# A state-space scan beside local attention on one core: the chunk scan for several state groups at once, the skip term added on eviction, softmax's maximum and sum by TensorE, and a new order

## The chip, the core and the metric

The kernel runs on one core of a Trainium2 chip. A core has five engines that run side by side, each with its own list of instructions: TensorE (PE in the profile; PEld is its weight load), VectorE (DVE), ScalarE (ACT), GpSimd (POOL) and SyncE (SP). Matmuls write to PSUM, and another engine has to copy ("evict") them from there to SBUF. DMAs are issued by an engine's instruction stream and land some microseconds later. The metric is the device time in microseconds (us), lower is better.

## The reference

Two independent layers on 2048 positions of 448 features; their outputs stand side by side. Layer A is a diagonal state-space recurrence with 448 complex states, layer B is causal, dilated local attention with 16 heads of 28 features, a window of 8 and a dilation of 2.

```python
def _A_ref(x, Lambda_re, Lambda_im, B_re, B_im, C_re, C_im, log_dt, Dskip):
    Lam = Lambda_re + 1j * Lambda_im
    Lam_bar = jnp.exp(jnp.exp(log_dt) * Lam)
    B_bar = ((Lam_bar - 1.0) / Lam)[:, None] * (B_re + 1j * B_im)
    Bu = jnp.einsum("bld,pd->blp", x + 0j, B_bar)
    for t in range(L):
        h = Lam_bar[None, :] * h + Bu[:, t, :]
        hs.append(h)
    return 2.0 * jnp.einsum("blp,dp->bld", hseq, C_re + 1j * C_im).real + x * Dskip[None, None, :]

def _B_ref(x, wqkv, wo):          # H = 16 heads, Dh = 28, W = 8, dilation 2
    q, k, v = ...                  # x @ wqkv by heads
    idx = pos[:, None] - (jnp.arange(W) * dil)[None, :]
    logits = jnp.einsum("bhsd,bhswd->bhsw", q, kg) * Dh ** -0.5   # kg, vg: k, v gathered at idx
    logits = jnp.where(mask, logits, -1e9)
    o = jnp.einsum("bhsw,bhswd->bhsd", softmax(logits), vg)
    return o.reshape(B, S, D) @ wo

out = jnp.concatenate([a, b], axis=-1)     # bf16, [1, 2048, 896]
```

## The kernel before

**How the order comes about.** The program is first described as a list of units, each with an engine (or a choice of ACT or VectorE), a cost, and the units it depends on. A table of numbers, `ORDER`, then gives the order in which the units are written out, and with it each engine's list of instructions; `BANKS` gives the PSUM buffer of each unit that needs one. So what stands ahead of an instruction on its engine is fixed by these tables. PSUM holds two tiles of two banks (ring "W") and four of one bank (ring "s").

**Layer A.** The 2048 positions are 128 chunks of 16. States come in seven groups of 64, real and imaginary parts on 128 partitions. The setup computes powers of the transition (exponential and sine on ACT, small VectorE operations up to L942), a table of turns per chunk (L952 to L967), and the folded input matrices Bcat (L996). The scan then does for each group m in turn:

- input matmuls into `scP` (two banks, positions 0 and 2 of every four) and `scb` (two single banks, 1 and 3), L1063;
- a short tree over the 16 positions of a chunk: ACT copies `eP` (L1076), matmul L1080, copy `e1` (L1084), matmul L1087, copy `eG` (L1091), matmuls L1095 to L1097. The last 128 columns of `scb` are then the sum over each chunk;
- the scan over the 128 chunks on VectorE: each column is turned by the table into a frame where the transition is real (L1103 to L1106, four instructions), scanned (L1107) and turned back into `pbuf` (L1109 to L1112). Nine instructions on 128 columns for each group;
- the carry of each chunk's start into its positions: matmuls L1117, L1123, L1124 and L1163 on PSUM that still holds its own part or is given it again by an ACT copy (L1131, L1149: "seed"), and evictions to `h`.

The output y is seven matmuls of 448 columns for each of the 16 positions (L1244), in pairs of positions in one W tile. An ACT copy puts the skip term, x times Dskip (product on VectorE, L1227), in the tile beforehand (L1256), the matmuls add to it, and ACT or VectorE evicts it.

**Layer B.** x comes by DMA transposes and the projection weights by loads (`load`, `wload`). Half of the weights are copied to the other half of the partitions (`shift`, L240) so that odd features can be multiplied. `proj` (L493) projects K and Q in two halves of 1024 positions, evicted by ACT or VectorE; Q's eviction scales. For a third block of columns two pieces are moved by DMAs on the SP queue (L555, L556). Fourteen products of q and shifted k (L578, 128x4096 on VectorE) go through matmuls that sum over a head's features into logits (L592). Softmax, once for each half: maximum over the window (L611), subtraction (L612), exponential on ACT (L618, ahead of it a table load L617), sum (L623), reciprocal (L624), product (L626), then a small merge (L635) and a transpose (L640). The attention weights are expanded on VectorE (L698, sixteen of 128x2176), multiplied with V on TensorE (`o_ps`, L709 and L714), evicted to oT, multiplied with wo (L734) and written out.

**Queues.** The SP queue issues x of both layers, then the wv weights, the moves of the third block and the outputs. The ACT queue issues the Q and K weights and two of A's three parameters; log_dt goes on SP between B's transposes.

Of the kernel before, what the change touches and what calls it, by code (L numbers as in the profile page):

```python
# [40 lines left out]
NHO = 3  # L41
NF = 3
# [3 lines left out]
ORDER = [  # L46
# [24 lines left out]
]  # L71
BANKS = [
# [154 lines left out]
class Ctx:  # L227
# [41 lines left out]
    def consts2(self):  # L269
# [38 lines left out]
        def masks():  # L308
            G.memset(mrow[:], 0.0)
# [6 lines left out]
        self.u_mask = self.plan.add("POOL", 1.5, masks, [self.boot], 1)  # L316
# [438 lines left out]
class PartA:  # L755
# [83 lines left out]
    def setup(self):  # L839
# [110 lines left out]
        def t1():  # L950
# [6 lines left out]
            for c in (6.28125, 1.9353071795864769e-03):  # L957
                V.scalar_tensor_tensor(a[:], k, -c, a[:], op0=ALU.mult, op1=ALU.add)
# [420 lines left out]
```

## Time and profile before

| | us |
|---|---|
| three runs | 141.83, 141.04, 143.16 |
| median | 141.83 |
| the profiled execution | 141.83 |
| its span | 139.8 |
| its mean granted TensorE clock | 0.988 of full speed |

The span is what the profile covers; 2.03 us of the profiled execution lie outside of it. The profile's stages, VectorE's timeline, the groups and the waits are shown with the prediction.

### The profile page before, as it was taken

To read this page: it belongs to the slowest core of one execution; us is meant where nothing else is said; L and a number is where in the kernel's file an instruction comes from. 1 tells how busy PE (TensorE), PEld (TensorE's weight loads), DVE (VectorE), ACT (ScalarE), POOL (GpSimd) and SP (SyncE) were. 2 spreads that over 40 slices of the span, in tenths; PEclk is the share of its full clock that TensorE was granted. 3 is DMA by queue.
4 is the path that set the end of the run, shared out by engine and by line. 5 is a ranking of instruction groups with operands and counts; after the bars stand their busy time and mean duration, and the time that the engine had idled before them with its cause. 6 is when DMAs were issued, how large, how long until landed. Compare 5 with 4: busy or idle time off the path is not lost.

```text
span 139.8 us, 2787 instructions
## 1 busy us (share of the span) xinstructions
PE 126.5 (91%) x1079; PEld 62.0 (44%) x1079; DVE 108.7 (78%) x176; ACT 105.8 (76%) x162; POOL 8.7 (6%) x46
## 2 busy tenths in 40 slices
PE   6499999999999999989897799799997999979980
PEld 2165753644343343543434355446454545535530
DVE  1348999999998999999999999999979748110360
ACT  0346999999999989679597989799986957545510
POOL 7890000000000000000000000000000000000000
PEclk9959999999999999999999999999999999999999
DMA  4999991796453458703600000300179272203345
GB/s 91 260 244 171 223 114 38 172 209 83 93 111 66 96 148 130 119 0 85 150 0 0 0 5 0 99 0 5 10 220 266 71 225 90 86 0 99 99 158 171
DMA packets 36484, 14.69 MB, mean 105 GB/s; under 512 B 26615, under 2 KB 36471, under 8 KB 36471
## 3 DMA queue, kind: packets, MB, share of 16 engines
q1 hardware_dynamic: 35549, 13.71, 45.3%
q10 hardware_dynamic: 922, 0.81, 2.3%
q8 instruction: 8, 0.13, 0.4%
q14 instruction: 5, 0.04, 0.1%
HBM read 5.57 MB, written 3.67 MB: 66 GB/s over the span
## 4 chain that ended last, share of the span: by engine, by line
PE 56%; DVE 19%; ACT 13%; issue 5%; SPq 4%; DMA 0%; DVEq 0%; ACTq 0%
PE y_ps L1244 14%; PE qk_ps L493 12%; PE wo_ps L734 6%; PE scb L1063 4%; PE scP L1063 4%; ACT qk L236 4%; SPq L390 4%; DVE prods L698 4%; DVE turned L1105 3%; DVE turned L1111 3%; ACT qk L238 3%; PE v_ps L664 3%; ACT V L236 2%; DVE turned L1107 2%; PE logits L592 2%
## 5 line engine op out<-in xcount | busy, mean ns | idle before, releaser
L578 DVE TENSOR_TENSOR prods<-qk 128x4096 bf16<-128x4096 bf16 x14 | 31.5, 2286 | 1.0 <-ACT qk L238 0.7
L493 PE MATMUL qk_ps<-rb 128*128 128x256 bf16 (+2 forms) x132 | 24.0, 338 | 2.1 <-DMA prm<-in_A_log_dt_dram 2.0
L698 DVE TENSOR_TENSOR prods<-at,band 128x2176 bf16<-128x2176 bf16 x16 | 19.9, 1285 | 0.0
L493 PEld LDWEIGHTS <-rb 128*128 128x128 bf16 (+1 forms) x132 | 11.5, 102 | 12.1 <-issue 6.9
L734 PE MATMUL wo_ps<-wo_p,oT 128*128 128x448 bf16 x64 | 14.4, 352 | 0.0
L1244 PE MATMUL y_ps<-Ccat,qk 128*128 128x448 bf16 x60 | 13.8, 352 | 0.0
L240 DVE CAST qk<-y_ps 128x896 bf16<-128x896 f32 (+1 forms) x4 | 3.9, 975 | 12.6 <-PE y_ps L1244 7.3
L1063 PE MATMUL scb<-xaT_sb,Bcat 128*128 128x512 bf16 (+1 forms) x56 | 13.6, 381 | 0.0
L1063 PE MATMUL scP<-xaT_sb,Bcat 128*128 128x512 bf16 (+1 forms) x56 | 13.6, 380 | 0.0
L664 PE MATMUL v_ps<-wv,rb 128*128 128x448 bf16 (+1 forms) x64 | 13.2, 353 | 0.2 <-ACT V L236 0.2
L1063 PEld LDWEIGHTS <-Bcat 128*128 128x128 bf16 (+1 forms) x112 | 8.6, 97 | 10.6 <-issue 3.6
L236 ACT CAST qk<-wo_ps 128x448 bf16<-128x448 f32 x12 | 6.5, 548 | 8.8 <-PE wo_ps L734 8.8
L1244 PE MATMUL y_ps<-Ccat,rb 128*128 128x448 bf16 x45 | 11.0, 353 | 0.0
L236 ACT CAST qk<-qk_ps 128x512 bf16<-128x512 f32 (+3 forms) x13 | 8.8, 693 | 1.2 <-PE qk_ps L493 1.2
L238 ACT ACTIVATE qk<-qk_ps 128x1024 bf16<-128x1024 f32 (+3 forms) x10 | 8.4, 857 | 0.6 <-PE qk_ps L493 0.6
L236 ACT CAST oT<-o_ps 128x512 bf16<-128x512 f32 x14 | 7.8, 606 | 1.2 <-PE o_ps L714 1.2
L734 PEld LDWEIGHTS <-oT 128*128 128x128 bf16 x64 | 6.2, 98 | 5.6 <-issue 0.5
L1244 PEld LDWEIGHTS <-qk 128*128 128x128 bf16 x60 | 5.9, 98 | 5.5
L664 PEld LDWEIGHTS <-rb 128*128 128x128 bf16 (+1 forms) x64 | 4.9, 96 | 6.7 <-issue 3.7
L236 ACT CAST V<-v_ps 128x448 bf16<-128x448 f32 x16 | 7.8, 545 | 0.1
L592 PE MATMUL logits<-prods,Zsel 128*32 128x512 bf16 (+1 forms) x112 | 7.5, 382 | 0.0
L1256 ACT CAST y_ps<-xaT_sb 128x896 f32<-128x896 bf16 x8 | 7.3, 914 | 0.2
(163 smaller groups left out, 212.0 us busy)
## 6 DMA issues: line engine op xcount, KB each, us to landing
out_dram<-qk SPq DMA_DIRECT2D x18, 112.0 KB, 2.0
xaT_sb<-in_A_x_dram SPq DMA_DIRECT2D x4, 448.0 KB, 5.7
out_dram<-qk SPq DMA_DIRECT2D x7, 224.0 KB, 2.1
rb<-in_B_wqkv_dram ACTq DMA_DIRECT2D x2, 336.0 KB, 4.0
wv<-in_B_wqkv_dram SPq DMA_DIRECT2D x2, 336.0 KB, 4.3
qk<-qk SPq DMA_DIRECT2D x4, 128.0 KB
bX<-in_A_B_re_dram SPq DMA_DIRECT2D x1, 392.0 KB
bX<-in_A_B_im_dram SPq DMA_DIRECT2D x1, 392.0 KB, 5.8
```

The source lines that it names most:

```text
L236: nc.scalar.copy(out, in_)
L238: nc.scalar.mul(out, in_, scale)
L390: nc.sync.dma_start(self.xB[:, b, j], x[256 * (4 * b + j):256 * (4 * b + j + 1)].rearrange("(n e) d -> n (e d)", e=2), transpose=True)
L493: nc.tensor.matmul(out(e)[:, NCH * j0:NCH * j1], lhsT=w, rhs=self.xB[rows, b, j0:j1, c, :], start=e not in begun, stop=True, skip_group_ch ...
L578: V.tensor_tensor(p, q[:, :, t0:t0 + HB].unsqueeze(1).to_broadcast([NCH, 4, 2, HB]), bass.AP(k.tensor, k.offset, [k.ap[0], [2, 4], [LDK, 2 ...
L592: nc.tensor.matmul(lg[32 * i:32 * i + 32, 4 * xx:4 * xx + 4, :], lhsT=sel[:, H - H * r:3 * H - H * r], rhs=pr[rows, :, g // 4, NCH * (g % ...
L664: nc.tensor.matmul(box[e][:], lhsT=self.xB[rows, b, jj, c, :], rhs=self.wv[rows, c, :], start=e not in begun, stop=True, skip_group_check= ...
L698: V.tensor_tensor(p.rearrange("p (g r v) -> p g r v", g=16, v=W), self.at[b][:, 64 * e + 16 * g:64 * e + 16 * g + 16].unsqueeze(2).to_broa ...
L734: nc.tensor.matmul(ps[:], lhsT=self.oT[:, ub["r"], kt, NCH * m:NCH * m + NCH], rhs=self.wo_p[:, kt, :], start=(kt == 0), stop=(kt == KT - 1))
L1063: mt(ps(i), lhsT=lhsT, rhs=rhs, start=i not in begun, stop=True, **kw)
L1244: nc.tensor.matmul(ps, lhsT=self.pb[:, m, PAD:] if j + jj == T - 1 else self.h[m][:, i, g * NCH:(g + 1) * NCH], rhs=self.Ccat[:, m, :], st ...
L1256: nc.scalar.copy(jb["y"][:, :, 0:D], self.xd[j])
```

## The change

- **The scan in two phases.** Part 1 does the input matmuls and the tree for each group and leaves the own parts in `h` straight away (no separate `eP`, `e1`, `eG`); the chunk sums go to a tile `sums` in fp32 by an ACT copy. `chunks(0, 4)` then turns, scans and turns back four groups at once, `chunks(4, 7)` the other three: turns are four instructions on 512 or 384 columns, the scan stays one instruction for each group. Part 2 does the carry of each group: an ACT copy seeds PSUM from `h` again, or (for three groups' two-bank part) VectorE adds PSUM to `h` (L1155). `h` of the first four groups has a tile of its own; that of the others lies in rb. Ccat moves into rb, oT into qk's region.
- **The skip term** is added by VectorE as it evicts y (L1244), and all of these evictions are VectorE's; the eight ACT copies go.
- **Softmax.** The maximum is kept in bf16 and subtracted by two matmuls with minus the identity; the sum is eight matmuls with the identity into `sm_ps`, which the reciprocal reads.
- **The table of turns** is made with fewer passes, and its sine with another scale.
- **Start.** All A parameters go on the ACT queue, and the Q weights on the SP queue behind four of B's transposes. K's projection of the first half is split by transposed block, the weight copies are three for each kind, and 13 warm-up matmuls stand where there were 10.
- **Order and banks** are new throughout.

```diff
-WARM = 10
-FIN = (("seed", "seed"), ("seed", "seed"), ("seed", "seed"), ("hold", "seed"), ("seed", "seed"), ("seed", "seed"), ("hold", "hold"))
+NB = 4
+WARM = 13
+FIN = (("add", "seed"),) * 3 + (("seed", "seed"),) * 4
...
-        self.more = lambda: nc.scalar.dma_start(self.wqk[:, 0:3, 0:D],
-                                                self.B_wqkv[0:DF, 0:D].rearrange("(k p) c -> p k c", p=NCH))
+        nc.sync.dma_start(self.wqk[:, 0:3, 0:D], self.B_wqkv[0:DF, 0:D].rearrange("(k p) c -> p k c", p=NCH))
...
         def top():
-            V.tensor_tensor(lg[:], lg[:], box["mx"][:].unsqueeze(1).to_broadcast([NCH, W, NCH]), op=ALU.subtract)
+            box["mx"] = pool.tile([NCH, NCH], bf16, name="mx", tag="mx")
+            V.tensor_reduce(box["mx"][:], self.lg[b][:].rearrange("p w q -> p q w"), axis=AX.X, op=ALU.max)
+
+        def sub():
+            for k in range(2):
+                nc.tensor.matmul(self.lg[b][:, 4 * k:4 * k + 4, :], lhsT=cx.minus[:],
+                                 rhs=box["mx"][:].unsqueeze(1).to_broadcast([NCH, 4, NCH]), start=False, stop=True,
...
+        def add():
+            box["sm"] = self.psum.tile([NCH, NCH], f32, name="sm_ps", slot=s_sm)
+            for w in range(W):
+                nc.tensor.matmul(box["sm"][:], lhsT=cx.ident[:], rhs=box["e"][:, :, w], start=(w == 0), stop=(w == W - 1))
+
         def norm():
-            V.tensor_reduce(sm[:], box["e"][:], axis=AX.X, op=ALU.add)
-            V.reciprocal(sm[:], sm[:])
+            V.reciprocal(sm[:], box["sm"][:])
...
-            V.tensor_scalar(k, a[:], 1.0 / TWO_PI, MAGIC, op0=ALU.mult, op1=ALU.add)
-            V.tensor_scalar(k, k, MAGIC, None, op0=ALU.subtract)
-            for c in (6.28125, 1.9353071795864769e-03):
-                V.scalar_tensor_tensor(a[:], k, -c, a[:], op0=ALU.mult, op1=ALU.add)
+            V.tensor_scalar(k, a[:], MAGIC, MAGIC, op0=ALU.add, op1=ALU.subtract)
+            V.tensor_tensor(a[:], a[:], k, op=ALU.subtract)
...
+        def chunks(m0, m1):
+            k = m1 - m0
+            x, u, w = xs[:, m0:m1], sc[:, 0, 0:k], sc[:, 1, 0:k]
+            tc, ts = (self.tab[:, i, m0:m1] for i in range(2))
+
+            def turn(out, op):
                 V.tensor_tensor(u, x, tc, op=ALU.mult)
+                for a, b in ((lo, hi), (hi, lo)):
                     V.tensor_tensor(w[a], x[b], ts[b], op=ALU.mult)
+                V.tensor_tensor(out, u, w, op=op)
+
+            def fore():
+                turn(u, ALU.add)
+                for i in range(k):
+                    V.tensor_tensor_scan(x[:, i], self.o["ex"][:, m0 + i, NLP:NPW].to_broadcast([NCH, NCH]), u[:, i], 0.0,
+                                         op0=ALU.mult, op1=ALU.add)
...
+                    if mode == "add":
+                        V.tensor_tensor(dst, src(box[name]), dst, op=ALU.add)
...
+        for m0, m1 in ((0, NB), (NB, NM)):
+            for m in range(m0, m1):
+                part1(m)
+            chunks(m0, m1)
+        for m in range(NM):
+            part2(m)
...
-                cx.copy(eng, o, jb["y"][:, j0:j1, 0:D])
-
-            def seed(j=j, jb=jb):
-                jb["y"] = self.psum.tile([NCH, 2, 512], f32, name="y_ps", slot=jb["s"])
-                nc.scalar.copy(jb["y"][:, :, 0:D], self.xd[j])
+                nc.vector.tensor_tensor(o, jb["y"][:, j0:j1, 0:D], self.xd[j][:, j0:j1], op=ALU.add)
...
-            en = lambda n: (("ACT", "DVE"), (act(n) + 0.13 * (n > 512), vec(n)))
+            en = lambda n: ("DVE", vec(n))
```

The order shows what moved. VectorE ahead of the first products (`prods<-qk`), before; `sh` to `spair`, `pw` and `Gd` are A's setup:

```order
L958 SCALAR_TENSOR_TENSOR ang_232<-tab,ang_232 128x896 x2
L924 TENSOR_TENSOR sh<-sh 128x84
L925 TENSOR_SCALAR sh<-sh 128x84
L927 TENSOR_TENSOR la<-sh,pex 128x14
L929 TENSOR_SCALAR la<-la,turn 128x7 x2
L931 TENSOR_TENSOR ab<-la,ll 128x28
L934 TENSOR_TENSOR gs<-ab 128x2x7x2
L937 TENSOR_TENSOR spair<-pex,sh 128x42x2 x2
L1012 TENSOR_TENSOR pw<-Dm,spair 128x640
L942 TENSOR_TENSOR Gd<-Dm,gs 128x896
L578 TENSOR_TENSOR prods<-qk 128x4096
```

The same place now, where lines have new numbers:

```order
L931 TENSOR_TENSOR Dm<-ident 128x64
L583 TENSOR_TENSOR prods<-qk 128x4096 x2
L937 TENSOR_TENSOR sh<-sh 128x84
L938 TENSOR_SCALAR sh<-sh 128x84
L940 TENSOR_TENSOR la<-sh,pex 128x14
L942 TENSOR_SCALAR la<-la,turn 128x7 x2
L944 TENSOR_TENSOR ab<-la,ll 128x28
L947 TENSOR_TENSOR gs<-ab 128x2x7x2
L950 TENSOR_TENSOR spair<-pex,sh 128x42x2 x2
L1024 TENSOR_TENSOR pw<-Dm,spair 128x640
L955 TENSOR_TENSOR Gd<-Dm,gs 128x896
```

Two products stand ahead of that part of the setup, and the passes of the table of turns stand further back. VectorE around a chunk scan, before, where `turned` is the scratch tile:

```order
L578 TENSOR_TENSOR prods<-qk 128x4096
L1103 TENSOR_TENSOR turned<-scb_764,tab 128x128
L1105 TENSOR_TENSOR turned<-scb_764,tab 64x128 x2
L1106 TENSOR_TENSOR turned<-turned 128x128
L1107 SCALAR_TENSOR_TENSOR turned<-pex,turned 128x128
L1109 TENSOR_TENSOR turned<-turned,tab 128x128
L1111 TENSOR_TENSOR turned<-turned,tab 64x128 x2
L1112 TENSOR_TENSOR pbuf<-turned 128x128
L1012 TENSOR_TENSOR pw<-Dm,spair 128x640
```

And now, with the scratch in qk's region, up to the second softmax (`mx` its maximum, `sm` its reciprocal):

```order
L583 TENSOR_TENSOR prods<-qk 128x4096 x2
L1113 TENSOR_TENSOR qk<-sums,tab 128x512
L1115 TENSOR_TENSOR qk<-sums,tab 64x512 x2
L1116 TENSOR_TENSOR qk<-qk 128x512
L1121 SCALAR_TENSOR_TENSOR sums<-pex,qk 128x128 x4
L1113 TENSOR_TENSOR qk<-sums,tab 128x512
L1115 TENSOR_TENSOR qk<-sums,tab 64x512 x2
L1116 TENSOR_TENSOR pbuf<-qk 128x4x128
L615 TENSOR_REDUCE mx<-logits 128x128
L713 TENSOR_TENSOR prods<-at_145,band 128x2176
L241 CAST own<-scb 128x128 x3
L713 TENSOR_TENSOR prods<-at_145,band 128x2176 x2
```

Four groups' sums stand ahead of one batch that stands behind the last product; the reciprocal (L637) is the next row. ACT at the second exponential, before:

```order
L1084 CAST e_937<-scb_901 128x512
L236 CAST rb<-scb_905 128x512
L618 ACTIVATE ex_sb<-logits 128x1024
L1091 CAST eG<-scb_918 128x384
L1076 CAST eP<-scP 128x1024
```

And now, where `own` is the tile of the first four groups' states:

```order
L1173 CAST scb<-own 128x384 x2
L237 CAST own<-scb 128x256 x4
L237 CAST own<-scb 128x128
L1094 CAST rb<-scP 128x2x512
L1144 CAST scb<-own 128x512
L627 ACT_TABLE_LOAD
L627 ACTIVATE ex_sb<-logits 128x1024
L1100 CAST rb<-scb_1061 128x512
```

A table load stands at this exponential, and the copies of part 2 of the first groups ahead of it.

More of the change, by code (lines that the diff above doesn't have):

```diff
@@ L769, in load @@
             src = (self.A_Lre, self.A_Lim, self.A_logdt)[i]
-            (nc.sync if i == 2 else nc.scalar).dma_start(self.prm[i * NM:(i + 1) * NM],
+            nc.scalar.dma_start(self.prm[i * NM:(i + 1) * NM],
                                                          src.rearrange("(m q) -> m q", q=PL).unsqueeze(1).to_broadcast([NM, 2, PL]))
-        load(0)
-        load(1)
-        self.b.more()
-        load(2)
+        for i in range(3):
+            load(i)
         nc.scalar.preload_act_table_set("natural_log_exp_and_others")
@@ L979, in setup @@
         self.u_s = a6
-        u = P.add("DVE", 4.0, t1, [a4], -1)
-        u = P.add("ACT", 3.2, t2, [u, a5], -1)
-        self.u_tab = P.add("DVE", 1.05, t3, [u], -1)
+        u = P.add("DVE", 3.1, t1, [a4], -1)
+        u = P.add("ACT", 3.8, t2, [u, a5], -1)
+        self.u_tab = P.add("DVE", 1.2, t3, [u], -1)
     def setup_weights(self, prio):
@@ new lines, in part1 @@
+            dx = [self.u_bc[m], u_pad]
+            ux = lambda i: [self.u_x[j] for j in range(i, T, 4)]
+            pr, pc = prio + m * 0.1, PRI["ch"] + m * 0.1
+            free = [] if m < NB else qk_done[0]
+            a = [P.add("PE", pe(3, 512), lambda i=i: bf(i), dx + ux(i), pr, acq=sl["P"]) for i in (0, 2)]
+            a.append(P.add("PE", pe(1, 512), lambda: br(0), dx + ux(0) + ux(2) + [self.u_xx[2]], pr, mode="r", acq=sl["P"]))
+            eP = P.add("ACT", act(1024), lambda: nc.scalar.copy(h[:, 0::2, :], box["P"][:]), a + free, pc, rel=sl["P"])
@@ new lines, in part1 @@
+            q = [P.add("PE", pe(3, 512), lambda i=i: bf(i), dx + ux(i), pr, acq=sl[i]) for i in (1, 3)]
+            q.append(P.add("PE", pe(1, 512), lambda: br(1), dx + ux(1) + ux(3) + [self.u_xx[3]], pr, mode="r",
+                           acq=(sl[1], sl[3])))
+            self.u_in += a + q
+            u = P.add("PE", pe(2, 512), s1, [eP, *q, u_pw], pc)
+            e1 = P.add("ACT", act(512), lambda: nc.scalar.copy(h[:, 1, :], box[1]), [u], pc, rel=sl[1])
+            u = P.add("PE", pe(1, 512), s2, [e1], pc)
@@ new lines, in part1 @@
+            e3 = P.add("ACT", act(384), lambda: nc.scalar.copy(h[:, 3, 0:384], box[3][:, 0:384]), [u], pc)
+            u = P.add("PE", 0.18, s3, [e3], pc)
+            u = P.add("ACT", act(128), lambda: nc.scalar.copy(xs[:, m], box[3][:, 384:512]), [u, self.u_tab], pc, rel=sl[3])
+            sums[m] = (u, eP, e1, e3)
+        def chunks(m0, m1):
[3 more added lines that the diff above has]
+            def turn(out, op):
@@ L1112, in chunks @@
-                V.tensor_tensor(pb[:, PAD:PAD + NCH], u, w, op=ALU.subtract)
-            last = pb[:, PAD - 1:PAD - 1 + NCH]
-            def s4(box=box, L=L, last=last):
-                for g in range(3):
-                    mt(box[3][:, g * NCH:(g + 1) * NCH], lhsT=L(4 * g + 4), rhs=last, start=False, stop=True, **kw)
-            def ev3(box=box, hget=hget):
-                nc.scalar.copy(hget()[:, 3, 0:384], box[3][:, 0:384])
-            def carry(out, lt, hv, new, last=last):
-                mt(out[:, 0:NCH], lhsT=lt, rhs=last, start=new, stop=True, **kw)
-                mt(out[:, NCH:512], lhsT=lt, rhs=hv[:, 3, 0:384], start=False, stop=True, **kw)
@@ L1140, in ev1f @@
-            def ev1f(eng, box=box, hget=hget, m1=m1):
-                if m1 == "add":
-                    nc.vector.tensor_tensor(hget()[:, 1, :], box[1], box["e1"][:], op=ALU.add)
-                else:
-                    cx.copy(eng, hget()[:, 1, :], box[1])
-            def back(eng, box=box, sl=sl, mP=mP):
-                box["P"] = self.psum.tile([NCH, 2, 512], f32, name="scP", slot=sl["P2"])
-                if eng == "ACT":
-                    nc.scalar.copy(box["P"][:], box["eP"][:])
-                else:
-                    for i in range(2):
-                        mt(box["P"][:, i, :], lhsT=cx.ident[:], rhs=box["eP"][:, i, :], start=True, stop=False, **kw)
@@ L1154, in p2 @@
-            def p2(box=box, sl=sl, mP=mP):
-                if mP == "add" and "P2" not in box:
-                    box["P"] = box["P2"] = self.psum.tile([NCH, 2, 512], f32, name="scP", slot=sl["P2"])
-                return box["P"]
-            def s6(L=L, hget=hget, carry=carry, p2=p2, mP=mP):
-                carry(p2()[:, 0, :], L(1), hget(), mP == "add")
-            def s7(L=L, hget=hget, p2=p2, mP=mP):
-                mt(p2()[:, 1, :], lhsT=L(1), rhs=hget()[:, 1, :], start=mP == "add", stop=True, **kw)
@@ L1176, in scan @@
-            ux = lambda i: [self.u_x[j] for j in range(i, T, 4)]
-            late = qk_done[m >= NHO]
-            a = [P.add("PE", pe(3, 512), lambda f=bf, i=i: f(i), dx + ux(i), pr, acq=(sl["P"], sl["fl"])) for i in (0, 2)]
-            a.append(P.add("PE", pe(1, 512), lambda f=br: f(0), dx + ux(0) + ux(2) + [self.u_xx[2]], pr, mode="r",
-                           acq=(sl["P"], sl["fl"])))
-            self.u_in += a
-            eP = P.add("ACT", act(1024), evP, a, pc, rel=None if hold else sl["P"])
@@ L1240, in y @@
             def y(jj, j=j, jb=jb, m0=0, m1=NM):
+                if "y" not in jb:
+                    jb["y"] = self.psum.tile([NCH, 2, 512], f32, name="y_ps", slot=jb["s"])
                 ps = jb["y"][:, jj, 0:D]
@@ L1261, in out @@
                     cx.ya_ring.put(jb["r"])
-            sl = jb["s"] = Slot("W", 1, 1)
+            sl = jb["s"] = Slot("W", 1)
             pc = pe(7, 448)
-            hs = [self.u_h[:20], self.u_h[20:24], self.u_h[24:]]
-            first = [P.add("ACT", act(896) + 0.04, seed, [self.u_xd[j]], pr, acq=sl)]
-            x = []
+            hs = [self.u_h[:25], self.u_h[25:30], self.u_h[30:]]
+            first, x = [], [self.u_xd[j]]
             if n < 3:
```

269 lines of the change are left out of this document (127 added, 142 removed), and 58 rows, old and new, of tables (BANKS, ORDER).

## The prediction

> **What bounds the kernel now.** I read the page's first part, then the chain by engine, then busy time by stage. In the stage rows the columns after the window are its length and, for PE, PEld, DVE, ACT and POOL, busy microseconds with the count of instructions; then the granted clock, the DMA share and GB/s.
> ```profile
> PE 126.5 (91%) x1079; PEld 62.0 (44%) x1079; DVE 108.7 (78%) x176; ACT 105.8 (76%) x162; POOL 8.7 (6%) x46
> PE 56%; DVE 19%; ACT 13%; issue 5%; SPq 4%; DMA 0%; DVEq 0%; ACTq 0%
> 0.00:21.00 21.00, 17.77 (x108) 10.03 (x108) 12.93 (x49) 12.00 (x17) 8.69 (x46) 0.92 1.02 184
> 21.00:60.00 39.00, 38.66 (x299) 16.57 (x301) 37.51 (x28) 36.89 (x57) 0.00 (x0) 1.00 0.60 113
> 60.00:113.50 53.50, 48.58 (x534) 24.42 (x527) 50.51 (x92) 45.84 (x75) 0.00 (x0) 1.00 0.25 63
> 113.50:139.80 26.30, 21.50 (x150) 10.94 (x147) 7.72 (x9) 11.06 (x15) 0.00 (x0) 1.00 0.35 116
> ```
> Over the span TensorE looks like the bound, but the stages say more: from 21 to 113.5 VectorE is busy for 88.0 of 92.5 us, and behind that it does little. Next I read VectorE's timeline at both ends of this stretch, and the end of the chain.
> ```profile
> 21.05 2.29 DVE L578 TENSOR_TENSOR prods<-qk 128x4096 bf16<-128x4096 bf16 x1
> ...
> 102.95 0.29 DVE L1103 TENSOR_TENSOR turned<-scb,tab 128x128 f32<-128x128 f32 x1 [0.71 <-PE scb L1097]
> ...
> 109.43 1.09 DVE L1227 TENSOR_TENSOR xaT_sb<-xaT_sb,dskip 128x1792 bf16<-128x1792 bf16 x1 [0.82 <-DMA xaT_sb<-in_A_x_dram]
> 110.44 0.62 DVE L240 CAST qk<-wo_ps 128x448 bf16<-128x448 f32 x1
> 110.98 2.48 DVE L698 TENSOR_TENSOR prods<-at,band 128x2176 bf16<-128x2176 bf16 x2
> 129.72 5.30 PE y_ps L1244 x28
> 135.81 0.53 ACT qk L236
> ```
> VectorE goes from its first product (21.05) to its last expansion (ends 113.46) with 2 to 3 us of waits in all. The last output product, wo products and y products need that expansion and run on TensorE behind it; the program ends 26.3 us after it. So I forecast the end of the last expansion, E, and add 26.3. I keep the 26.3: the new order leaves about 113 matmuls of 448 columns behind it, 113 x 0.189 us (5.30 / 28 above) = 21.4, with 0.7 for the last output product and 4.2 from TensorE's end (135.6) to the program's end, 26.3 again. Before, fewer matmuls stood there, but TensorE also came late.
>
> **The start, -5.5 us.** The Q weights leave the ACT queue for the SP queue, behind four x transposes, in the slot of the log_dt load.
> ```profile
> 6.23 0.53 SPq L770 DMA_DIRECT2D prm<-in_A_log_dt_dram  x1
> rb<-in_B_wqkv_dram ACTq DMA_DIRECT2D x2, 336.0 KB, 4.0
> L240 DVE COPY rb<-rb 64x1344 bf16<-64x1344 bf16 x2 | 1.9, 930 | 5.2 <-DMA rb<-in_B_wqkv_dram 5.2
> L240 DVE CAST qk<-y_ps 128x896 bf16<-128x896 f32 x3 | 3.3, 1091 | 8.4 <-PE y_ps L1244 7.3 <-issue 1.0
> 10.26 0.17 DVE L907 TENSOR_TENSOR den<-pf 128x7 f32<-128x7 f32 x1
> ...
> 11.64 0.39 DVE L469 COPY wm<-rb 128x896 bf16<-128x896 bf16 x1
> 18.10 0.24 DVE L924 TENSOR_TENSOR sh<-sh 128x84 f32<-128x84 f32 x1
> ```
> 6.23 + 4.0 gives 10.2; I take 10.4. VectorE then does two weight copies (1.9), the wm copy (0.3 net of overlap), K's eviction (1.1), the odd copy (0.5) and nine small operations (10.26 to 11.64, 1.4): 15.6, and I take 15.5 for the first product. Before, VectorE did the whole setup first, to 21.05; of it the block from 18.10 (2.95) now stands behind two products, and most of the 5 us table of turns later still. Bounds for this gain: 7 (nothing behind the weights costs) and 3 (Q's projection, and not VectorE, sets 18.0).
>
> **VectorE's work between the two points, +0.7.** Start-to-start times are used, since neighbours overlap by about 0.1.
> ```profile
> 63.76 0.28 DVE L1103 TENSOR_TENSOR turned<-scb,tab 128x128 f32<-128x128 f32 x1
> ...
> 66.61 0.48 DVE L1012 TENSOR_TENSOR pw<-Dm,spair 128x640 bf16<-128x640 bf16 x1
> 67.01 1.22 DVE L611 TENSOR_REDUCE mx<-logits 128x128 f32<-128x1024 f32 x1
> 68.26 1.23 DVE L612 TENSOR_TENSOR logits<-logits,mx 128x1024 f32<-128x1024 f32 x1
> 69.40 0.48 DVE L1012 TENSOR_TENSOR pw<-Dm,spair 128x640 bf16<-128x640 bf16 x1
> L623 DVE TENSOR_REDUCE sm<-ex_sb 128x128 f32<-128x1024 bf16 x2 | 2.4, 1214 | 0.0
> ```
> Gone: a chunk scan takes 2.85 (63.76 to 66.61), seven take 19.95. Batched, a 128x512 operation of this kind lies between 0.28 (128 columns) and 1.23 (1024 columns): 0.70 on that line, 0.57 for 384. Eight and eight of these with seven scans of 0.46 give 13.4, so -6.6. Two subtractions (68.26 to 69.40, 1.14 each) and two sums (1214 ns, as long as the maximum that takes 67.01 to 68.26, so 1.25 each): -4.8. Two of four skip products leave the stretch (-2.0), and one wo eviction (-0.6). Together -14.0. Moved in: the setup block 2.95; the shorter table 3.0 (three passes of 896 columns, at most 1.1 each on the line above); three PSUM additions of 128x1024 in the place of ACT copies, 3.5 by the 1.14 row; evictions that the order gives to VectorE: four of 512 columns 2.4, V 0.5, two of 256 0.7, four of 128 1.0, odd and B copies 0.7, together 5.3. That is 14.75, net +0.7. The bound is the batched size: at the small form's 0.28 for 128 columns with no saving it would be 1.12, so +6.7; at 0.50 it is -3.
>
> **The waits that the batch makes, +1.1.** One chunk scan needed one group's sums; now the first needs four, and whatever stands behind it on VectorE (the second maximum, expansions, casts of own) waits too.
> ```profile
> L578 DVE TENSOR_TENSOR prods<-qk 128x4096 bf16<-128x4096 bf16 x14 | 31.5, 2286 | 1.0 <-ACT qk L238 0.7
> PE scb L1117 <- DVE pbuf L1112: 4.5, 6, 1.0
> 23.38 0.61 SPq L556 DMA_DIRECT2D qk<-qk  x1
> ...
> 36.12 5.12 SPq L806 DMA_TRANSPOSE xaT_sb<-in_A_x_dram  x4
> xaT_sb<-in_A_x_dram SPq DMA_TRANSPOSE x16, 3.4
> ```
> The SP queue carries A's x transposes behind the copy that waits for VectorE's scaling of q3. That comes at about 15.5 + 8.6 = 24.1, near the 23.38 of before; 17 steps of 1.28 (5.12 / 4) behind it put the last transpose's issue at 44.4 and its landing, with 3.4, at 47.8. TensorE gets there at about 47.6 by its own work (an estimate from the columns of its list at full clock); some 13.1 us of columns and 2.8 of mode changes and evictions follow to the fourth group's sums, 63.7. VectorE's own list reaches that point 46 us behind its first product, 61.5. The wait is 2.2; the 1.0 of idle time before L578 and 0.1 more that lie in that place now go, so +1.1. Bounds: -1.1 (no wait) and +5. The 4.5 us that TensorE waits for pbuf go too, but I give nothing for them: TensorE's own list ends earlier than VectorE's here, so they become a wait for an expansion.
>
> **The second softmax, +1.8.** Behind its maximum VectorE does three expansions and three casts, 4.2 us, and then wants the reciprocal. Meanwhile ACT has some 6.0 in its list: by the rows below (V's casts take 0.49 for 448 columns) four casts of 256 columns 1.1 and one of 128 0.2, one of 1024 1.0, a seed of 512 0.6, the load 1.28, the exponential 1.02; and TensorE's new sum with what lies around it 0.8.
> ```profile
> 43.37 0.97 ACT L236 CAST V<-v_ps 128x448 bf16<-128x448 f32 x2
> 44.36 1.28 ACT L617 ACT_TABLE_LOAD   x1
> 45.65 1.02 ACT L618 ACTIVATE ex_sb<-logits 128x1024 bf16<-128x1024 f32 x1
> ```
> The load is new at this place, since the second sine comes between the two exponentials. It took 1.28, and the exponential began right behind it. The Trainium skill ("ScalarE: Activation LUTs", What ACT_TABLE_LOAD costs) adds about 1.38 us of drain to a load of about 1.28, so 2.66 per switch. By it the forecast would rise by 1.4, to 139.8. The row shows no such drain: the cast ahead ended at 44.34 and the exponential came at 45.65. The bounds of this term are 0.5 (the casts wait behind it) and 3.2.
>
> **Waits that go, -1.5.** The 0.71 at 102.95 (a group's sums, now ready long before) and the 0.82 at 109.43 (the skip load, now needed after E). What is late next there is the expansion's own list, so I count both fully.
>
> **At no cost.** Eight ACT seeds of y go (below), the sums and subtractions on TensorE add 1.7 us of columns where part 1 drops 1.7: cover is VectorE, the later engine. The skip term moves into VectorE's evictions:
> ```profile
> L1256 ACT CAST y_ps<-xaT_sb 128x896 f32<-128x896 bf16 x8 | 7.3, 914 | 0.2
> ```
> Of this I expect nothing, since VectorE has little behind 113.5; per pair TensorE needs 14 x 0.189 = 2.65, VectorE 1.09 for the eviction, 0.5 of a skip product and 0.3 to be told, 1.9.
>
> **Sum.** -5.5 + 0.7 + 1.1 + 1.8 - 1.5 = -3.4. E becomes 110.1, the span 136.4. The profiled execution took 141.83 with a span of 139.8, the 2.03 outside stay, and it is itself the median of the three runs (141.04 to 143.16): 138.4.
>
> **Rivals.** The bound is then VectorE, TensorE and ACT within a microsecond of each other from 80 to 111, so unnamed waits decide much.
> No gain: the early start is eaten. Against it speaks that VectorE's list is full from 15.5 on; for it that the batch's wait depends on the last of 17 SP steps and on TensorE, which do not start earlier. If the wait is 5 and the reciprocal's 3.2, -5.5 + 0.7 + 3.9 + 3.2 - 1.5 = +0.8, 142.6; with half of the excess, 140.5.
> The load at the second exponential costs twice its row, since ACT must first run empty: 1.28 more on a path without slack, 139.7. Against it speaks the row without a gap. This is the case that the Trainium skill's rule above describes.
> TensorE as the bound: VectorE keeps ahead, and of TensorE's 13.3 us without work (139.8 - 126.5) the 4.5 of pbuf and some 3.5 at the start and at expansions go: 141.8 - 8.0 = 133.8, about 134.
> Slower: with VectorE alone evicting y, each of the two W slots is free only when VectorE is through. If its chain per pair exceeds TensorE's 2.65, six pairs each expose the chain's eviction and hop, 1.36: 6 x 1.36 = +8.2, 146.6. That decides once the half skip product and the wo casts stand in front of the eviction too; by the 1.9 above it does not.
>
> **How the numbers follow.** Forecast case 138.4 (136.5 to 140.2) has 0.56; no gain, about 140.5 to 142.6, 0.21; the longer load 0.03; TensorE-bound, 134, 0.10; slower, 146, 0.10. Two per cent, about what a measurement of this kernel can tell from no change, is 139.0 below and 144.7 above. Of the forecast case 0.38 lies below 139.0 and 0.18 above; with 0.10 that makes 0.48 faster; 0.18 + 0.21 + 0.03 make 0.42 within; 0.10 slower. The range 135.0 to 141.8 leaves out 0.05 below, and 0.14 above.
>
> **What would show it.** Right: the first product at 15.5, the chunk multiplication of 512 columns at 0.70, a wait of about 2 before it on the fourth group's sums, one of 1.8 before the second reciprocal, the last expansion ending near 110 and the end 26 us behind. Wrong: a first product after 18, a wait before the batch over 5, or VectorE waiting for nothing between and TensorE busy to the end; in the tail, y matmuls that wait for VectorE's evictions.

## The result and the profile after

The changed kernel is slower: 1.047 times the time of the kernel before, 95% interval 1.037 to 1.057 (median 149.65 us of four runs, 147.22 to 150.83; the kernel before 141.44 beside it). Two of the four runs, those with the lowest granted TensorE clock (0.957 and 0.973), are left out of the ratio, so it is not the ratio of the two medians; the profile below is of one of them (150.46 us), and a second profile of the same kernel stands under the experiments. The forecast was 138.4 us, range 135.0 to 141.8.

The page's first part, the chain by engine, and busy time by stage (the columns are those of the prediction):

```profile
PE 132.7 (89%) x1145; PEld 66.1 (44%) x1145; DVE 110.4 (74%) x153; ACT 92.8 (62%) x157; POOL 8.7 (6%) x48
PE 51%; ACT 24%; DVE 7%; SPq 7%; issue 6%; DMA 3%; ACTq 0%; DVEq 0%
0.00:21.00 21.00, 18.48 (x153) 11.30 (x154) 13.25 (x44) 12.88 (x20) 8.72 (x48) 1.00 1.03 205
21.00:60.00 39.00, 34.36 (x267) 15.43 (x265) 31.68 (x33) 29.89 (x42) 0.00 (x0) 1.00 0.49 99
60.00:113.50 53.50, 51.59 (x517) 25.19 (x516) 47.39 (x59) 44.24 (x87) 0.00 (x0) 0.97 0.22 61
113.50:148.70 35.20, 28.28 (x213) 14.18 (x211) 18.03 (x19) 5.81 (x11) 0.00 (x0) 0.93 0.29 94
```

From 21 to 60 us all three engines work less than before: VectorE 31.7 us where it was 37.5, TensorE 34.4 for 38.7, ACT 29.9 for 36.9. Nobody is the bound there; they wait for each other. The stretch behind 113.5 is 35.2 us where it was 26.3. ACT's share of the chain went from 13% to 24%, and VectorE's from 19% to 7%.

VectorE's timeline, the places of the prediction, with the wait ahead of each row in brackets:

```profile
15.15 4.49 DVE L583 TENSOR_TENSOR prods<-qk 128x4096 bf16<-128x4096 bf16 x2
...
26.70 4.49 DVE L583 TENSOR_TENSOR prods<-qk 128x4096 bf16<-128x4096 bf16 x2 [2.28 <-ACT qk L237]
33.88 6.70 DVE L583 TENSOR_TENSOR prods<-qk 128x4096 bf16<-128x4096 bf16 x3 [2.69 <-ACT qk L237]
...
69.20 0.69 DVE L1113 TENSOR_TENSOR qk<-sums,tab 128x512 f32<-128x512 f32 x1 [0.85 <-ACT sums L1104]
...
84.92 0.96 DVE L637 RECIPROCAL sm<-sm_ps 128x128 f32<-128x128 f32 x1 [2.58 <-PE sm_ps L633]
...
94.02 0.62 DVE L241 CAST V<-v_ps 128x448 bf16<-128x448 f32 x1 [1.17 <-PE v_ps L679]
...
113.83 3.68 DVE L713 TENSOR_TENSOR prods<-at,band 128x2176 bf16<-128x2176 bf16 x3
```

The first product starts at 15.15, almost as forecast (15.5). But the third waits 2.28 for an ACT eviction and the fifth 2.69. The last expansion ends at 113.83 + 3.68 = 117.5, not 110.1, and the end comes 31.2 us behind it, not 26.3.

The next table takes VectorE's timelines apart in the same way for every kernel of this study; the rows with a plus stand on top of split and swap together. The waits are all bracketed times between the first product and the last expansion; work is what is left between the two points; the tail is the span less the end of the last expansion.

| kernel | first product | waits | work | last expansion ends | tail | span |
|---|---|---|---|---|---|---|
| before | 21.05 | 2.75 | 89.7 | 113.5 | 26.3 | 139.8 |
| forecast | 15.5 | 4.2 | 90.4 | 110.1 | 26.3 | 136.4 |
| changed | 15.15 | 12.2 | 90.2 | 117.5 | 31.2 | 148.7 |
| changed, again | 14.8 | 12.35 | 89.7 | 116.9 | 29.5 | 146.4 |
| split | 14.85 | 7.8 | 90.5 | 113.15 | 28.85 | 142.0 |
| swap | 14.9 | 11.05 | 89.8 | 115.7 | 27.4 | 143.1 |
| split and swap | 15.2 | 7.8 | 90.5 | 113.6 | 26.9 | 140.5 |
| + table early (a) | 14.9 | 10.45 | 90.1 | 115.45 | 27.25 | 142.7 |
| + table early (b) | 15.0 | 9.3 | 90.0 | 114.4 | 27.2 | 141.6 |
| + turns group by group | 15.0 | 7.6 | 95.5 | 118.1 | 26.7 | 144.8 |
| + softmax on VectorE | 15.1 | 2.9 | 94.6 | 112.6 | 26.7 | 139.3 |
| + sum alone on VectorE | 15.1 | 4.6 | 92.9 | 112.7 | 26.6 | 139.3 |

So the work that the forecast priced came out to 0.2 us. What it missed are 8 us of waits and 5 us of tail. (The forecast's 4.2 is 2.2 for the batch, 1.8 for the second reciprocal and 0.15 left over.)

### The profile page after: what moved, and what is told of

Its sections match the earlier page's. It is cut to its first block, busy times and chain, and to the rows that moved or that the text cites. A ratio compares the mean times of both kernels' runs of the same rounds, so it can differ in the third digit from the quotient of the medians.

```text
span 148.7 us, 2887 instructions
## 1 busy us (share of the span) xinstructions
PE 132.7 (89%) x1145; PEld 66.1 (44%) x1145; DVE 110.4 (74%) x153; ACT 92.8 (62%) x157; POOL 8.7 (6%) x48
## 4 chain that ended last, share of the span: by engine, by line
PE 51%; ACT 24%; DVE 7%; SPq 7%; issue 6%; DMA 3%; ACTq 0%; DVEq 0%
PE y_ps L1236 14%; SPq L392 6%; ACT qk L237 6%; PE wo_ps L749 5%; PE qk_ps L497 5%; PE scP L1067 5%; DVE prods L583 5%; PE scb L1067 4%; PE v_ps L679 4%; PE logits L597 3%; DMA rb<-in_B_x_dram 3%; ACT own L237 3%; PE sm_ps L633 3%; ACT qk L239 2%; ACT rb L237 2%
## 5 line engine op out<-in xcount | busy, mean ns | idle before, releaser
L237 ACT CAST qk<-wo_ps 128x448 bf16<-128x448 f32 x13 | 7.7, 638 | 23.1 <-PE wo_ps L749 23.1
L497 PE MATMUL qk_ps<-rb 128*128 128x128 bf16 (+3 forms) x168 | 21.2, 288 | 0.7 <-DMA rb<-in_B_x_dram 0.7
L1244 DVE TENSOR_TENSOR qk<-y_ps,xaT_sb 128x896 bf16<-128x896 f32 (+1 forms) x9 | 8.9, 986 | 9.3 <-PE y_ps L1236 9.1
L1236 PE MATMUL y_ps<-rb,own 128*128 128x448 bf16 x60 | 14.8, 372 | 0.0
L679 PE MATMUL v_ps<-wv,rb 128*128 128x448 bf16 (+1 forms) x64 | 14.7, 383 | 0.0
L749 PE MATMUL wo_ps<-wo_p,qk 128*128 128x448 bf16 x64 | 13.9, 352 | 0.0
L1236 PE MATMUL y_ps<-rb 128*128 128x448 bf16 x45 | 11.6, 367 | 0.0
L237 ACT CAST qk<-o_ps 128x512 bf16<-128x512 f32 x13 | 8.5, 713 | 1.6 <-PE o_ps L729 1.6
L1236 PEld LDWEIGHTS <-own 128*128 128x128 bf16 x60 | 6.0, 103 | 6.0 <-issue 1.4
L1236 PEld LDWEIGHTS <-rb 128*128 128x128 bf16 x45 | 4.5, 101 | 4.5 <-issue 0.7
```

The lines of the kernel that those rows point to most:

```text
L237: nc.scalar.copy(out, in_)
L497: nc.tensor.matmul(out(e)[:, NCH * j0:NCH * j1], lhsT=w, rhs=self.xB[rows, b, j0:j1, c, :], start=e not in begun, stop=True, skip_group_ch ...
L679: nc.tensor.matmul(box[e][:], lhsT=self.xB[rows, b, jj, c, :], rhs=self.wv[rows, c, :], start=e not in begun, stop=True, skip_group_check= ...
L749: nc.tensor.matmul(ps[:], lhsT=self.oT[:, ub["r"], kt, NCH * m:NCH * m + NCH], rhs=self.wo_p[:, kt, :], start=(kt == 0), stop=(kt == KT - 1))
L1236: nc.tensor.matmul(ps, lhsT=self.pb[:, m, PAD:] if j + jj == T - 1 else self.h[m][:, i, g * NCH:(g + 1) * NCH], rhs=self.Ccat[:, m, :], st ...
L1244: nc.vector.tensor_tensor(o, jb["y"][:, j0:j1, 0:D], self.xd[j][:, j0:j1], op=ALU.add)
```

## Experiments

### The changed kernel again

> The changed kernel as it is, to have a second profile of it beside the experiments. In the first one TensorE's granted clock fell to about half in two stretches (85.5 to 89.2 and 130 to 133.8 us), each right behind a stretch in which TensorE had waited; that is worth about 3 us of its 148.7. If the half clock is an accident of that execution, this one has a span of 145 to 146 and everything else alike: third product at 26.7 after a wait of 2.3, fifth at 33.9 after 2.7, TensorE's wait of 2.0 at 129. If it belongs to the waits, it is there again.

Median 149.36 us, ratio 1.049 (1.044 to 1.054). The span is 146.4: TensorE's wait of 1.99 in the tail and VectorE's of 2.28 and 2.69 are there again to the hundredth. The half clock is not: TensorE's seven matmuls behind the wait took 1.48 where they took 1.71, and the next seven 0.92 + 0.73 where they took 1.70 + 1.32. There is one fall elsewhere instead, from 40 to 43 us. So the clock accounts for 1.7 us of the first profile's tail (31.2 against 29.5) and for none of these three waits. Smaller waits do differ: the one of 1.17 for V, behind the fall at 86 us, is absent here, and the first reciprocal's is 1.63 for 0.69.

### Products in two halves, and the written order at the last position of y

The split, for the first half's products:

```diff
-                    V.tensor_tensor(p, q[:, :, t0:t0 + HB].unsqueeze(1).to_broadcast([NCH, 4, 2, HB]),
-                                    bass.AP(k.tensor, k.offset, [k.ap[0], [2, 4], [LDK, 2], [1, HB]]), op=ALU.mult)
+                    for e in range(2):
+                        V.tensor_tensor(p[:, :, e], q[:, e, t0:t0 + HB].unsqueeze(1).to_broadcast([NCH, 4, HB]),
+                                        bass.AP(k.tensor, k.offset + e * LDK, [k.ap[0], [2, 4], [1, HB]]), op=ALU.mult)
```

> Each of the first half's seven products of 128x4096 is written as two of 128x2048, one for even and one for odd positions. Theory false wait: the strided read of one 128x4096 product covers, as an interval, columns of K and Q that belong to the second half, so it waits for second-half evictions on ACT that were written ahead of it, though it needs none of them. Then the third product starts at about 24.4 (26.7), the two waits of 2.3 and 2.7 on ACT's qk evictions shrink to under 1 together, the last expansion ends 3.5 to 4.5 us earlier and the kernel is that much faster, less 7 x 0.06 for the added instructions. Rival late evictions: ACT's list is full from 12.5 to 28, the products' own operands are late, and the waits stay: the time stays within 1 us. Rival batch: the early waits go, but the first batch of four groups then waits for the sums instead, since these hang on TensorE and on A's x transposes: its wait grows from 0.85 to 3 or more and the kernel gains under 2 us.

The swap, in the table of the order (585 is the last position's y, 586 the eviction of the position before it):

```diff
-    584, 549, 586, 585, 588,
+    584, 549, 585, 586, 588,
```

> Two neighbours in the written order change places, the matmuls of the last position's y and the eviction of the position before it, which share a two-bank tile in PSUM. Every engine's list stays the same; only the wait of the one for the other goes. Theory: this wait (TensorE 2.0 at 129, the matmuls with pbuf waiting for VectorE's eviction of the other bank, which stands behind a wo eviction, a skip product and another eviction) is most of the tail's excess, so the time falls by 2.0, and by up to 3.5 where the half clock behind the wait goes too. Rival: TensorE only waits at the next tile instead (for VectorE's eviction of W0, done at 127.4), and the gain is under 0.7.

> The split products and the swap together. If the two waits are separate, the gains add: 5.5 to 7 us from the changed kernel, 140 to 143 us, about level with the kernel before. If the split's gain is taken back in the middle by the batch's wait, 2 to 4 us. If TensorE is the next bound in the tail, the sum is less than the parts.

Measured: split 144.86 us, swap 144.93, both together 142.33, against 149.36 of the changed kernel beside them and 141.42 of the kernel before. Both together are level with the kernel before: 1.003 (0.998 to 1.009). The swap alone stands at 1.029 (1.021 to 1.037). The profiled executions have spans of 142.0, 143.1 and 140.5 against 146.4, and the sizes below are read from these.

VectorE's timeline of the split kernel:

```profile
23.91 2.34 DVE L584 TENSOR_TENSOR prods<-qk 128x2048 bf16<-128x2048 bf16 x2
27.04 9.17 DVE L584 TENSOR_TENSOR prods<-qk 128x2048 bf16<-128x2048 bf16 x8 [0.79 <-DMA qk<-qk]
...
65.60 0.69 DVE L1118 TENSOR_TENSOR qk<-sums,tab 128x512 f32<-128x512 f32 x1 [0.85 <-ACT sums L1109]
...
81.31 0.96 DVE L642 RECIPROCAL sm<-sm_ps 128x128 f32<-128x128 f32 x1 [2.57 <-PE sm_ps L638]
```

The third product starts at 23.91 without a wait, and both waits on ACT are gone; what is left is 0.79, now for the moved piece of the third block. The last expansion ends 3.7 us earlier, though the added instructions cost VectorE 0.8 of work. So the operands had been there all along. In the changed kernel ACT's row that the third product waited for, and the product, stand like this:

```profile
26.07 0.59 ACT L237 CAST qk<-qk_ps 128x512 bf16<-128x512 f32 x1
26.70 4.49 DVE L583 TENSOR_TENSOR prods<-qk 128x4096 bf16<-128x4096 bf16 x2 [2.28 <-ACT qk L237]
```

The wait in the built program points to exactly this eviction. It writes 512 of K's columns of the second half of the positions. The product reads two pieces of 518 columns of the first half, for even and odd positions, which start 1034 columns apart, and the 512 lie in the gap of 516 between them. As one access with a stride the product's range takes them in; as two accesses it doesn't. Rival "late evictions" falls. So does rival "batch": the batch came 4.5 us earlier than beside it (65.60 for 70.11) and still waited 0.85.

TensorE's timeline around the last position of y (matmuls with pbuf), first of the changed kernel, with the VectorE eviction of the tile's other bank between its rows, then of the swapped one:

```profile
126.53 0.73 PE L1236 MATMUL y_ps<-rb 128*128 128x448 bf16 x3
128.57 0.62 DVE L1244 TENSOR_TENSOR qk<-y_ps,xaT_sb 128x448 bf16<-128x448 f32 x1
129.25 1.71 PE L1236 MATMUL y_ps<-rb,pbuf 128*128 128x448 bf16 x7 [1.99 <-DVE qk L1244]
```

```profile
124.71 0.73 PE L1236 MATMUL y_ps<-rb 128*128 128x448 bf16 x3
125.27 1.49 PE L1236 MATMUL y_ps<-rb,pbuf 128*128 128x448 bf16 x7
```

The eviction ends at 129.19 and the matmuls, which write the other bank, begin at 129.25. With the swap no engine's list changed, and the wait is gone, with nothing in its place: the tail falls by 2.1 us (29.5 to 27.4). That answers the rival of a wait at the next tile. The rest of the swap's gain (the last expansion ends 1.2 earlier in it) lies ahead of the edit, in the waits of the first softmax: the first reciprocal's is 1.63 in the changed kernel's second profile, where the clock fell from 40 to 43 us, and 0.69 in this one. It is not the edit's. The edits' own parts, 3.7 and 2.1, add up: the two together have 5.9 us less of span.

### The table of turns earlier

Units of the order are moved: 30 (the table's VectorE passes), 31 (its sines on ACT, ahead of 203, the first exponential) and 196 (a product of the second half, ahead of 205, the first reciprocal). This is (a); in (b) 30 stands behind 176, the third product, and 31 behind 164, an eviction of Bcat further ahead.

```diff
     178,
+    30,
...
+    31,
     203,
...
+    196,
     205,
...
-    30,
...
-    31,
...
-    196,
```

> On top of split and swap together (span 140.5, time 142.3): the table of turns is made earlier, its VectorE passes right behind the seventh product and its sines on ACT ahead of the first exponential, and one product of the second half goes ahead of the first reciprocal. That takes two of ACT's five table loads away (1.28 each), that of the second sine and that of the second exponential. Theory load: the wait of 2.6 before the second reciprocal is to about half this load, so it falls to about 1.3, the last expansion ends 1.3 earlier, TensorE's wait for that exponential (1.2) falls too and with it the half clock behind it; time 140 to 141. Rival: the exponential of the second half waits for its maximum and for TensorE's subtraction anyway, and the wait stays over 2. Second rival: the first softmax now comes later, because the sines (3.7 us of ACT) stand ahead of it, and the first reciprocal waits 2 or more; then nothing is won.

> As the one before, but the passes of the table stand behind the third product and the sines on ACT some ten instructions further ahead. Theory load: the same 1.3 at the second reciprocal; the first reciprocal waits less than there, but evictions of the second half's keys and of V stand behind 5 us of ACT and products or TensorE may wait for them. Between 139 and 143.

Measured: (a) 144.13 us, 1.007 (1.002 to 1.013), and (b) 143.32 in its one run, with the kernel before at 142.94 on that chip. VectorE's timeline of (a):

```profile
49.00 0.96 DVE L642 RECIPROCAL sm<-sm_ps 128x128 f32<-128x128 f32 x1 [3.01 <-PE sm_ps L638]
...
54.18 0.23 DVE L653 TENSOR_TENSOR at_k<-mg_ps,at_k 128x64 bf16<-128x64 f32 x1 [1.96 <-PE mg_ps L650]
...
59.91 4.49 DVE L588 TENSOR_TENSOR prods<-qk 128x4096 bf16<-128x4096 bf16 x2 [1.50 <-PE logits L602]
```

The load was what the theory said: without it the wait before the second reciprocal is 1.20 in both versions, 1.38 less. But the second rival held too. The sines now stand ahead of the first exponential, and the first softmax waits 3.01, 1.96 and 1.50 where it waited 0.70, 0.58 and 0.17. (TensorE's clock was at half from 49 to 53 us of this profile, so the 1.96 need not be the edit's alone; the 3.01 lies ahead of it.) In (b) the first maximum waits 2.23 for TensorE instead, and the first reciprocal 1.49. Nothing is won.

### The chunk scan's turns group by group, and the softmax on VectorE

```diff
             def turn(out, op):
-                V.tensor_tensor(u, x, tc, op=ALU.mult)
...
+                for i in range(k):
+                    V.tensor_tensor(u[:, i], x[:, i], tc[:, i], op=ALU.mult)
...
```

> On top of split and swap together: the turns of the chunk scan are done group by group again, in the same place and order, so 4 instructions on 128x512 become 16 on 128x128 (and on 384 columns 12). It tells what the batching saves by itself. By the rows of the kernel before (0.31 from start to start) a batch of four takes 32 x 0.31 + 4 x 0.34 = 11.3 and one of three 8.5, where the batched ones took 7.7 and 6.3 in the profile: the last expansion ends 5 to 6 us later and the time rises by that. Rival: VectorE's waits behind the batch (2.6 at the reciprocal) take in a part, and it rises by 2 to 4.

One run, 146.54 us, 4.2 more than with the turns batched. VectorE's timeline, the first batch from its first instruction to the maximum behind it, group by group and then batched:

```profile
65.91 0.29 DVE L1119 TENSOR_TENSOR qk<-sums,tab 128x128 f32<-128x128 f32 x1 [0.68 <-ACT sums L1109]
...
76.19 1.22 DVE L620 TENSOR_REDUCE mx<-logits 128x128 bf16<-128x1024 f32 x1
```

```profile
65.27 0.69 DVE L1118 TENSOR_TENSOR qk<-sums,tab 128x512 f32<-128x512 f32 x1 [0.85 <-ACT sums L1109]
...
72.99 1.22 DVE L620 TENSOR_REDUCE mx<-logits 128x128 bf16<-128x1024 f32 x1 [0.65 <-PE logits L602]
```

10.3 us against 7.1 (72.99 less the wait of 0.65 less 65.27): in all VectorE's work is 5.0 us more, and the last expansion ends 4.5 later. Batching does what it should, and nearly all of it reaches the end, as far as one run can tell.

For the softmax, the two matmuls with minus the identity become one VectorE subtraction again, and the eight of the sum one reduce, in the same places:

```diff
-            for k in range(2):
-                nc.tensor.matmul(self.lg[b][:, 4 * k:4 * k + 4, :], lhsT=cx.minus[:],
...
+            V.tensor_tensor(self.lg[b][:], self.lg[b][:], box["mx"][:].unsqueeze(1).to_broadcast([NCH, W, NCH]), op=ALU.subtract)
...
-            for w in range(W):
-                nc.tensor.matmul(box["sm"][:], lhsT=cx.ident[:], rhs=box["e"][:, :, w], start=(w == 0), stop=(w == W - 1))
+            V.tensor_reduce(box["sm"][:], box["e"][:], axis=AX.X, op=ALU.add)
```

> On top of split and swap together: the maximum is subtracted by VectorE again (the matmuls with minus the identity go), and the sum over the window is VectorE's reduce again, in the same places. It tells what that part of the change brings. VectorE gets 2 x 1.14 and 2 x 1.25 more, 4.8. Theory: VectorE is the bound in the middle, so the last expansion ends later by 4.8 less what its waits at the two reciprocals (0.7 and 2.6) take in: 3 to 5 us. Rival: the path from the maximum to the reciprocal, and not VectorE's list, is what counts there; TensorE's way round costs hops that the old way has not, and the difference is under 2.

> The last kernel of the group before once more, timed against the kernel before: split and swap, subtraction and sum on VectorE. Theory level: moving them to TensorE took 4.2 us of work from VectorE and gave it 4.8 us of waits, so this kernel is as fast as the one with split and swap alone or up to 1 us faster, 0.98 to 1.00 of the kernel before. Rival: its single time was luck of the granted clock, and it lies at 1.00 to 1.01.

> The same with the subtraction on TensorE and only the sum on VectorE. If the waits came from the sum on TensorE (matmuls between the exponential and the reciprocal, of which eight take 2.0 us in the profile, and TensorE's own order around them), then VectorE's work falls by 2.3 and its waits rise by under 1: last expansion about 1.5 us earlier than in the kernel beside it, 0.97 to 0.99 of the kernel before. If they come from the exponential's place in ACT's list, the wait at the sum grows by what the subtraction saves, and the two kernels are level.

With both steps on VectorE: 141.28 in the first run, then 142.02 (median of twelve), 0.996 of the kernel before (0.992 to 1.000). With the sum alone on VectorE: 139.56 us (139.06 to 141.35), 0.982 (0.975 to 0.989). That last one is faster than both kernels of this case.

The reciprocal's wait on TensorE with split and swap; then the sum's wait, in the kernel with both steps on VectorE and in the one with the sum alone:

```profile
80.99 0.96 DVE L642 RECIPROCAL sm<-sm_ps 128x128 f32<-128x128 f32 x1 [2.58 <-PE sm_ps L638]
```

```profile
80.58 1.23 DVE L634 TENSOR_REDUCE sm_ps<-ex_sb 128x128 f32<-128x1024 bf16 x1 [0.40 <-ACT ex_sb L629]
```

```profile
79.57 1.23 DVE L637 TENSOR_REDUCE sm_ps<-ex_sb 128x128 f32<-128x1024 bf16 x1 [0.54 <-ACT ex_sb L632]
```

The theory (waits swallow less than the work) falls: moving both steps to TensorE took 4.1 us of work from VectorE and gave it 4.9 of waits. The table splits this: the sum's move took 2.4 of work and gave 3.2 of waits (split and swap beside the sum alone on VectorE), the subtraction's 1.7 of each. So the sum's move is the one that lost, by 0.8. The last run's expectation named it and missed the sizes: with the subtraction on TensorE it had under 1 us of added waits and a last expansion 1.5 earlier. The second exponential, with split and swap and then with the sum alone on VectorE:

```profile
77.89 1.02 ACT L632 ACTIVATE ex_sb<-logits 128x1024 bf16<-128x1024 f32 x1
```

```profile
78.51 1.02 ACT L632 ACTIVATE ex_sb<-logits 128x1024 bf16<-128x1024 f32 x1
```

With the sum on TensorE the reciprocal begins 2.1 us behind the exponential's end (80.99 less 78.91). As a reduce the sum begins 0.04 behind it (79.57 less 79.53) and takes 1.2, and the reciprocal begins 1.3 behind it, at 80.83. TensorE's rows in the changed kernel say why, eight matmuls of 128 columns each, and then six that also add into the same columns of PSUM, three by three:

```profile
46.93 1.98 PE L633 MATMUL sm_ps<-ex_sb,ident 128*128 128x128 bf16 x8
...
67.92 0.61 PE L653 MATMUL pt_at<-perm,at_k 128*128 128x128 bf16 x8
...
68.37 0.50 PE L1087 MATMUL scb<-own,pw 128*128 128x128 bf16 x6
```

The operand that streams is named first. The transpose's eight read perm's columns one behind the other; the sum's eight read every eighth element of ex_sb, and take 1.98 for 0.61. Adding into one place is not the price, since the six of L1087 do so at 0.50. The Trainium skill ("SBUF — State Buffer", "Door 1: The DMA port swizzle") says that SBUF is read in lines of 16 bytes and that each access that crosses to a new line pays; eight bf16 elements are 16 bytes, so here each does. The rows agree, though no run here changed the stride alone.

The last kernel's expansion ends no earlier in its profile than its neighbour's (112.7 and 112.6, both spans 139.3), while its runs are faster. Its profiled execution, 141.04, was one of its two slowest: the clock was at half from 82 to 85 us, 0.988 in the mean, where the neighbour's was 0.999. Among the executions with a mean clock of 0.995 and more, timed side by side, the spans are 137.3 to 137.9 with the sum alone on VectorE (four) and 138.6 to 139.3 with both steps there (three). By these the subtraction is worth moving, some 1.3 us; where in the program that shows, no profile tells.

## Why the prediction was wrong

**The start, -5.5.** Right as a time (15.15). Wrong as a gain. The rival "no gain" was set aside with "VectorE's list is full from 15.5 on", and that sentence is the step that failed: the list was full, but its third and fifth products waited 5.0 us for ACT, where the sum put the products' waits at nothing and even took off the 1.0 of before. I looked at what each product computes from, and not at what its access spans. With the split 3.7 us of the gain are there.

**VectorE's work, +0.7.** Right as a net: 0.5 measured (90.2 less 89.7), 0.0 in the second profile. A turn's operation of 512 columns took 0.69, forecast 0.70, and the batching's saving was shown by undoing it, 5.0 us of work. The sum had 6.6 for it; undone in the new place, a group's scan takes 2.57 (10.28 / 4) where it took 2.85. The softmax steps were worth 4.1 and not 4.8. Two savings that came out 2.3 smaller leave the net right only if what moved in cost some 2.5 less than the 14.75 (by difference, not measured), so part of the agreement is luck.

**The batch's wait, +1.1.** Mis-sized: 0.85 where 2.2 was forecast. The chain of 17 queue steps and TensorE's columns that led to 63.7 doesn't set it, since the wait stayed 0.85 when VectorE came to it 4.5 us earlier. (The chain also has a slip: 24.1 and 17 steps of 1.28 give 45.9, not 44.4, and it shows no row for its 2.8 of mode changes and evictions.) The traces show where it comes from: the product at 59.06 waits 0.17 for logits matmuls on TensorE, and from there TensorE works without a pause up to the sums (busy for all of the 10.5 us from 58.4 to 68.9). So the batch begins 10.1 us behind that product, at 69.20, as in the split kernel (55.45 and 65.60), while VectorE's own list takes 9.3.

**The second softmax, +1.8.** The right place, but 2.58. The load was half of it, as forecast (1.38 less without it). The term that was mis-sized is the sum on TensorE: with what lies around it, it was put at 0.8, and from the exponential's end to the reciprocal 2.1 us passed (82.85 to 84.92), 1.98 of them its matmuls. ACT's list was 0.5 shorter than forecast (4.7 for 5.2). By the Trainium skill's 2.66 for a switch ("ScalarE: Activation LUTs", What ACT_TABLE_LOAD costs) the load's removal should have brought 2.66; 1.38 is measured, 0.10 over the load's own 1.28.

**Waits that go, -1.5.** Right, both are gone; six new ones of 0.2 to 1.2 (an eviction of Q, the first reciprocal, the merge, a product, the second maximum, V) add 3.8, of which the forecast had none.

**Evicting y by VectorE alone, at no cost.** Wrong by 2.0, and not as the rival had it. VectorE's chain per pair is short enough: with split and swap TensorE's rows show no wait from the last expansion on, and the tail is 26.9 us against 26.3 before. The cost was one wait, between a matmul and the eviction of the other bank of its tile, which the written order set.

**The sum.** Work and start: right within 0.6. Waits +8.0, tail +4.9 of which about 1.7 is the profiled execution's clock. Forecast 136.4 of span, 148.7 measured. The bounds of the work term were added up wrong as well (+6.7 and -3 are about +6.2 and -2 by the same rows), which moved nothing.

## What to carry to other kernels

Before a start that comes earlier is counted as a gain, ask for every later instruction in that list what its access spans, and not only what it uses: here a strided read waited for an earlier-written write between its first and its last element, and a matmul for an earlier-written read of the other bank of its tile, though in both cases the columns are not the same. The built program holds these waits. Both vanished by splitting an access and by writing two lines in the other order, without moving anything on an engine. A step that is moved off the bound engine brings only what the way round doesn't cost: by the runs the subtraction was worth moving; the sum, read with a stride, was not.

## What was not expected of the hardware

Eight matmuls of 128 columns took 1.98 us with every eighth element read and 0.61 with neighbouring ones. TensorE's granted clock fell to about half for some 3 to 4 us in several executions, in the first profile 3.1 us behind a wait of TensorE of 1.2 and 1.1 us behind one of 2.0, in others elsewhere, and in some not at all (in the swapped kernel the same wait of 1.2 was followed by none). Executions of one kernel with and without it differ by 1 to 2 us.
